# One long branch per chunk of rows, or short ones: layer one of a mixture-of-experts kernel in four parts

## The chip, the core and the metric

One Trainium2 chip, one of its NeuronCores. Five engines run their own instruction streams and meet at semaphores: PE multiplies matrices, ACT and DVE compute element by element, POOL issues the row gathers and scatters, SP issues the other transfers. The metric is device time of one execution in microseconds (us). [...]

## The reference, cut to what matters

Eight batches of linear attention (random features, 8 heads, 576 positions) give 4608 rows of 512 numbers. Each row then goes to one of 8 experts, the one with the largest gate logit:

```python
for e in range(E):                       # E = 8
    mask = expert_idx == e
    xe = x[mask]                         # rows of 512
    h = np.maximum(xe @ w1[e], 0.0)      # w1[e]: 512 x 1024
    ye = h @ w2[e]                       # w2[e]: 1024 x 512
    out[mask] = gate_w[mask, None] * ye
```

How many rows an expert gets is known only when the kernel runs.

## The kernel before, in words

The first 310 us hold the attention, the routing, 256 rows of one expert and the first chunk. After that the experts' rows are taken in chunks of up to 384 (`T3`), t = 0, 1, 2, ...; a chunk belongs to one expert, and its last chunk holds what is left. The number of rows of chunk t lies in the flags as `r` (row 4), written by the routing; each engine loads it into a register (`reg`, L909) and branches on it.

A step (`step`, L1109) does chunk t. **Layer one** makes the 1024 hidden values in eight groups f of 128: 12 matmuls each for wide chunks (`l1`, L967: high and low parts of weights and rows), then ACT takes the relu and DVE the rest of it (`hid`, L992, L993). Chunks of at most 192 rows use `l1_both` (L974, L976: 8 matmuls per group, high and low rows side by side) and `hid_both`: ACT copies, DVE adds, ACT and DVE split (L1001, L1002, L992, L993). Four banks of PSUM (`p_1`) are used in turn, so a fifth group waits for the first one's `hid`. **Layer two** (`l2`) makes the output in blocks of 128 rows, 24 matmuls each (L886), or 16 where a block has at most 64 rows (L1029). Since each hidden group is one step of its sums, a block's last matmuls wait for the last group's `hid`. ACT scales the output (`out2`, L1080), POOL scatters it (L1061).

Beside it, the rows of chunk t+1 are brought into place: gathered by POOL (L923), reshaped through memory by SP (`move`, L942, L944), transposed by DVE and split by ACT and DVE (`xtrans`, L951, L57, L51), in three thirds. A wide chunk does a third after groups 1, 3 and 5; a slim chunk does all three ahead of its own layer one. Where the expert changes, ACT and DVE split the next weights (`change`: w1 when layer one has read the old ones, w2 at the start of the next step).

The size is chosen once per chunk (`cases`, L1034 to L1048): a tree of branches ends in one of six bodies, for 384, 320, 256, 192, 128 and 64 rows, each with all of layer one and all of layer two. The bodies stand one behind the other in every engine's stream, in that order. On PE a matmul stands as one row in the program and is two records in the trace, a weight load (PEld) and the matmul (PE). In such records with their closing branches the six bodies have 337, 322, 290, 210, 178 and 162, about 1,510 per chunk. The order of instructions on each engine is the order in which the code is written.

Of the kernel before, what the change touches and what calls it, by code (L numbers as in the profile page):

```python
# [18 lines left out]
P = 128  # L19
# [14 lines left out]
T2 = 2 * P  # L34
A3 = 3
T3 = A3 * P
HT = P // 2
# [7 lines left out]
ET = mybir.EngineType  # L45
# [371 lines left out]
class Routing:  # L417
# [99 lines left out]
    def step(self, name, product, f):  # L517

        v = {}
        def made(bank):  # L520
            v["o"] = product(bank)
        def step():
            if "o" not in v:
                made(self.bank(name))
            f(v["o"])
        step.product = made
        return step
# [263 lines left out]
class Experts:  # L791
# [2 lines left out]

    NC, NF, T2 = DM // P, F // P, T2
    WE = (ET.DVE, ET.Activation, ET.SP)

    def __init__(self, tc, ctx, rt, xs, w1, w2, out, ident, ps):
        self.tc, self.nc, self.ctx, self.rt, self.ps, self.ident = tc, tc.nc, ctx, rt, ps, ident
# [203 lines left out]
        for h, l, k in self.homes2(slice(f, f + w), n):  # L1003
            self.high_low(h, l, y[:, :, k])

    def wide(self, t, n):
        for f in range(self.NF):
            if t == 0:
                self.split(2, (f,))
            self.l1(t, f, n)  # L1010
            self.hid(f, n)
            if t > 0 and f in (1, 3, 5):
                self.xtrans(t + 1, f // 2)

    def slim(self, t, n):
        for a in range(A3):
            self.xtrans(t + 1, a)
        w = 2 if n <= P else 1
        for i in range(self.NF // w):
            for b in range(w):  # L1020
                self.l1_both(t, w * i + b, self.p_1[i % 4][:, b * 2 * n:(b + 1) * 2 * n], n)
            self.hid_both(i, w * i, w, n)

    def l2(self, a, half=False):
        s, p = slice(a * P, (a + 1) * P), self.p_2[a]
# [5 lines left out]
            else:  # L1031
                self.triple(p, self.hb[:, 0, c, s], self.hb[:, 1, c, s], c)

    def cases(self, r, first):  # L1034


        def body(n):
            first(n)
            a = (n - 1) // P
            self.l2(a, n % P > 0)  # L1040
            for b in range(a - 1, -1, -1):
                self.l2(b)

        self.either(r > T2, lambda: self.either(r > T3 - HT, lambda: body(T3), lambda: body(T3 - HT)),
                    lambda: self.either(r > T2 - HT, lambda: body(T2),
                                        lambda: self.either(r > P, lambda: body(T2 - HT),
                                                            lambda: self.either(r > HT, lambda: body(P),
                                                                                lambda: body(HT)))))  # L1048

    def either(self, cond, one, other):  # L1050
        with self.tc.If(cond) as c:
# [17 lines left out]
    def out2(self, t, a, r):  # L1069
        nc, p, g, i = self.nc, self.p_2[a], self.gate(t, a), A3 * t + a  # L1070

        def half(y):
            nc.scalar.copy(self.yt[:HT], p[HT:])
            nc.vector.tensor_tensor(out=self.yt[:HT], in0=p[:HT], in1=self.yt[:HT], op=ALU.add)
            nc.vector.tensor_scalar(out=y[:HT], in0=self.yt[:HT], scalar1=g[:HT], scalar2=None, op0=ALU.mult)

        def both():
            y = self.y()
            v = self.reg(4, t, T3, (ET.Activation, ET.DVE))
            self.either(v > a * P + HT, lambda: nc.scalar.activation(y, p, AF.Copy, scale=g), lambda: half(y))  # L1080
            self.scatter(y, self.idx[:, i:i + 1])

        if a:
            with self.tc.If(r > a * P):
                both()
        else:
            both()
# [5 lines left out]
    def change(self, t, n):  # L1093
        def f():
            self.split(n)
            self.next(t, n)
        self.when(self.reg(0, t, 1, self.WE), f)

# [8 lines left out]
        self.change(t, 1)  # L1107

    def step(self, t, following):  # L1109
        self.t = t  # L1110
        if 0 < t < NCH - 2:
            self.gather(t + 2)
        if t == 0:
            self.wide(t, T3)
            self.l21()
            for a in range(A3):
                self.xtrans(1, a)
            self.cases(self.reg(4, t, T3, (ET.PE,)), lambda n: None)
            self.gather(2)
            self.next(0, 2)  # L1120
        else:
            self.cases(self.reg(4, t, T3, (ET.PE, ET.Activation, ET.DVE)),
                       lambda n: self.wide(t, n) if n > T2 - HT else self.slim(t, n))
        if t + 1 < NCH:
            self.weigh(t + 1)
        self.nc.gpsimd.drain()
        following()
        r = self.reg(4, t, T3, (ET.Activation, ET.DVE, ET.Pool))
        for a in range(A3 - 1, -1, -1):
            self.out2(t, a, r)  # L1130
# [111 lines left out]
```

## Time and profile before

| | us |
|---|---|
| time, median of 3 runs | 724.16 (720.52 to 725.4) |
| profiled execution: its own time | 723.94 |
| its span, first to last instruction | 722.2 |
| PE busy | 671.8 (93%) |
| ACT / DVE / POOL busy | 363.9 / 380.8 / 267.2 |

The execution has 13 chunks. Their layer one starts on PE at 264 (t = 0), 311, 345, 381, 412, 447, 482, 516, 559, 579, 613, 647 and 695 us. By the shapes of the matmuls t = 3 takes the 320 body, t = 8 the 192 body, t = 12, the last, the 64 body, the ten others the 384 body.

How to read the rows: a line of the timeline has the start in us from the span's start, the length, engine, source line, operation, result and operands, how many were merged (x), and in brackets how long the engine was idle just before and what ended that. "issue" is idle time in which it waited for nothing that the profile shows. The DMA queue q8 of kind "instruction" carries PE's program.

### The profile page before, as it was taken

The page shows a single profiled execution, that of the slowest core. Times are in us where ns is not written, and L with a number is a line of the kernel's source. Part 1 is how long each engine was busy: PE and PEld are TensorE (multiplying, and loading weights), DVE is VectorE, ACT ScalarE, POOL GpSimd, SP SyncE. Part 2 cuts the span into 40 slices and gives each one's busy share as a digit, 9 for nine tenths or more (in the row PEclk, how much of TensorE's full clock was granted, in tenths as well). Part 3 has the DMA queues.
Part 4 walks back from the last instruction along what each step waited for, and adds up shares of the span by engine and source line. Part 5 has one row for each costly group of instructions (what it writes and reads, how often), then busy time and mean ns, then how long its engine had stood idle before and what let it go on. Part 6 is the DMA issues. An engine that isn't in the chain of part 4 may idle for free. (4 is left out here: it accounts for less than half of the span.)

```text
span 722.2 us, 18842 instructions
## 1 busy us (share of the span) xinstructions
PE 671.8 (93%) x7011; PEld 607.5 (84%) x7011; DVE 380.8 (53%) x789; ACT 363.9 (50%) x1142; POOL 267.2 (37%) x489
## 2 busy tenths in 40 slices
PE   8999999999999999999999998999994999999645
PEld 5999999999889879888979796989893997979545
DVE  4788888888878787331404560505542570505111
ACT  4999999999989564221312531213521551312110
POOL 5554557877777761331212032030033031221300
PEclk9999999999999999999999999999998999999956
DMA  7673653844852328643333465413366374313100
GB/s 211 205 224 93 214 178 101 256 131 142 272 210 71 96 63 248 228 130 105 108 74 104 132 210 163 122 63 95 135 202 168 91 277 142 97 54 90 49 4 8
DMA packets 92869, 100.54 MB, mean 139 GB/s; under 512 B 28702, under 2 KB 73246, under 8 KB 92064
## 3 DMA queue, kind: packets, MB, share of 16 engines
q1 hardware_dynamic: 85216, 79.27, 36.7%
q0 software_dynamic: 6800, 19.03, 8.2%
q8 instruction: 89, 1.46, 0.9%
q14 instruction: 76, 0.62, 0.3%
q10 hardware_dynamic: 688, 0.16, 0.1%
HBM read 72.12 MB, written 29.77 MB: 141 GB/s over the span
## 5 line engine op out<-in xcount | busy, mean ns | idle before, releaser
L967 PE MATMUL p<-xb,w1p 128*128 128x384 f32 (+1 forms) x1056 | 185.5, 335 | 9.3 <-issue 4.8
L967 PEld LDWEIGHTS p<-xb,w1p 128*128 128x128 f32 x1056 | 181.8, 189 | 13.9 <-issue 7.0
L1061 POOL DMA_INDIRECT out_dram<-ys,idx x38 | 38.2, 1004 | 349.6 <-ACT ys L1080 141.5
L993 DVE SCALAR_TENSOR_TENSOR hb<-p,hb 128x384 fp32r<-128x384 f32 (+1 forms) x88 | 46.9, 541 | 159.8 <-ACT hb L992 159.5
L886 PE MATMUL p<-w2p,hb 128*128 128x512 f32 x552 | 127.1, 389 | 0.0
L886 PEld LDWEIGHTS p<-w2p,hb 128*128 128x128 f32 x552 | 103.6, 188 | 21.5
L191 DVE TENSOR_REDUCE mx<-pp 128x8 f32<-128x1024 f32 x64 | 78.0, 1218 | 10.9 <-PE pp L185 10.2
L199 ACT ACTIVATE qp<-pp,mx 128x128 f32<-128x128 f32 x256 | 76.9, 432 | 0.0
L199 ACT ACTIVATE kp<-pp,mx 128x128 f32<-128x128 f32 x256 | 73.8, 382 | 5.7 <-DVE de L283 1.8
L185 PE MATMUL pp<-omt,th 64*128 64x128 f32 x1024 | 72.1, 281 | 0.2 <-ACT qp_-1_320 L199 0.2
L992 ACT ACTIVATE hb<-p 128x384 fp32r<-128x384 f32 (+1 forms) x88 | 41.3, 478 | 59.6 <-PE p L967 59.6
L185 PEld LDWEIGHTS pp<-omt,th 64*128 64x128 f32 x1024 | 63.4, 191 | 0.3 <-ACT qp_-1_320 L199 0.3
L1080 ACT ACTIVATE ys<-p,gt 128x512 f32<-128x512 f32 x23 | 15.8, 688 | 85.0 <-PE p L886 84.5
L886 PE MATMUL p_1tr<-w2p,hb 128*128 128x512 f32 x240 | 56.4, 390 | 0.0
L211 POOL TENSOR_TENSOR k<-kp 128x256 f32<-128x256 f32 x64 | 46.5, 727 | 25.8 <-ACT kp L199 20.8
L886 PEld LDWEIGHTS p_1tr<-w2p,hb 128*128 128x128 f32 x240 | 44.9, 188 | 9.0
L274 PE MATMUL nu<-kva,qt 128*64 128x73 f32 x1008 | 46.3, 233 | 0.7 <-issue 0.7
L176 DVE COPY th<-tr 128x512 f32<-128x512 f32 x63 | 43.3, 688 | 5.3 <-PE tr L168 3.2
L974 PE MATMUL p<-xb,w1p 128*128 128x384 f32 (+1 forms) x64 | 23.0, 424 | 24.8 <-issue 24.8
L243 ACT COPY qt<-t 128x512 f32<-128x512 f32 x64 | 41.9, 654 | 2.3 <-PE t L168 1.8
L274 PEld LDWEIGHTS nu<-kva,qt 128*64 128x64 f32 x1008 | 36.8, 136 | 5.1 <-issue 0.9
L225 PE MATMUL kf<-kp,v 128*64 128x128 f32 x512 | 39.7, 275 | 0.1
(386 smaller groups left out, 1087.4 us busy)
## 6 DMA issues: line engine op xcount, KB each, us to landing
w1s<-in_moe_w_dram SPq DMA_DIRECT2D x5, 2048.0 KB, 9.2
w2s<-in_moe_w_dram SPq DMA_DIRECT2D x5, 2048.0 KB, 10.5
xq<-chunk_rows SPq DMA_DIRECT2D x52, 192.0 KB, 4.2
v<-in_v_dram SPq DMA_DIRECT2D x32, 256.0 KB, 5.8
token_rows<-x SPq DMA_DIRECT2D x8, 1024.0 KB, 8.6
k<-in_k_dram SPq DMA_DIRECT2D x31, 256.0 KB, 5.3
q<-in_q_dram SPq DMA_DIRECT2D x31, 256.0 KB, 5.6
chunk_rows<-xgm SPq DMA_DIRECT2D x7, 768.0 KB, 3.6
```

What stands on the lines that cost most here:

```text
L176: self.nc.vector.tensor_copy(t.rearrange("p n (a t) -> p a n t", a=2), s[("tr", h)])
L185: nc.tensor.matmul(o[:, a, n, :], t[r, n, :], self.om[r], start=True, stop=True)
L191: self.nc.vector.tensor_reduce(out=mx, in_=s[("pp", h)], axis=AX.X, op=ALU.max, negate=True)
L199: self.nc.scalar.activation(o[:, j, :], p[:, a, 2 * n + i, :], AF.Exp, bias=mx[:, a, 2 * n + i:2 * n + i + 1])
L211: nc.gpsimd.tensor_tensor(out=k2, in0=kp[:, :2, :], in1=kp[:, 2:, :], op=ALU.add)
L225: nc.tensor.matmul(pkv[c * D:(c + 1) * D, :M], vv, kk, start=n < 2, stop=n > 2)
L243: self.nc.scalar.copy(qt.rearrange("p n (a t) -> p a n t", a=2), s[("t2", h)])
L274: nc.tensor.matmul(o[r, j, :], qt[:, j, r], kva[:, h if h >= 0 else 2 * j + a, :], start=True, stop=True)
L886: self.nc.tensor.matmul(p, x, w[:, c, :], start=c == 0 and x is h and w is self.w2h, stop=c == self.NF - 1 and x is l)
L967: self.nc.tensor.matmul(o, w[:, c, k], x[:, c, :], start=i == 0, stop=i == len(ops) - 1)
L992: self.nc.scalar.activation(h, p, AF.Relu)
L993: self.nc.vector.scalar_tensor_tensor(out=l, in0=p, scalar=0.0, in1=h.bitcast(F32), op0=ALU.max, op1=ALU.subtract)
```

## The change

The choice of a size is taken four times in layer one, once for two groups each (`layer1`, `choose`), and then again for each block of layer two (`layer2`). The body of a part is two groups at one of the six widths: 49 records (48 and a branch) at 384, 320 and 256 rows, 33 or 34 at 192, 128 and 64. A part is 246 records with its branches, layer two about 250, a chunk some 1,240. The thirds of `xtrans` follow parts 0, 1 and 3 at every width. Chunk 0 keeps its straight layer one (`first`) and loses two branches in `out2`.

```diff
-    def wide(self, t, n):
+    def first(self, n):
         for f in range(self.NF):
-            if t == 0:
-                self.split(2, (f,))
+            self.split(2, (f,))
+            self.l1(0, f, n)
+            self.hid(f, n)
+
+    def wide(self, t, g, n):
+        for f in (2 * g, 2 * g + 1):
             self.l1(t, f, n)
             self.hid(f, n)
-            if t > 0 and f in (1, 3, 5):
-                self.xtrans(t + 1, f // 2)
-
-    def slim(self, t, n):
-        for a in range(A3):
-            self.xtrans(t + 1, a)
+
+    def slim(self, t, g, n):
         w = 2 if n <= P else 1
-        for i in range(self.NF // w):
+        for f in range(2 * g, 2 * g + 2, w):
+            i = f + g // 2 if w == 2 else f
             for b in range(w):
-                self.l1_both(t, w * i + b, self.p_1[i % 4][:, b * 2 * n:(b + 1) * 2 * n], n)
-            self.hid_both(i, w * i, w, n)
+                self.l1_both(t, f + b, self.p_1[i % 4][:, b * 2 * n:(b + 1) * 2 * n], n)
+            self.hid_both(i, f, w, n)
...
-    def cases(self, r, first):
...
+    def layer1(self, t):
+        r = self.reg(4, t, T3, self.CE)
+        for g in range(self.NF // 2):
+            body = lambda n: self.wide(t, g, n) if n > T2 - HT else self.slim(t, g, n)
+            self.choose(r, [T3 - i * HT for i in range(T3 // HT)], body)
+            if g != 2:
+                self.xtrans(t + 1, (0, 1, None, 2)[g])
+
+    def choose(self, r, ns, body):
+        if len(ns) == 1:
+            return body(ns[0])
+        self.either(r > ns[1], lambda: body(ns[0]), lambda: self.choose(r, ns[1:], body))
+
+    def layer2(self, t):
+        r = self.reg(4, t, T3, (ET.PE,))
+        one = lambda a: self.l2(a) if t == 0 else \
+            self.either(r > a * P + HT, lambda: self.l2(a), lambda: self.l2(a, True))
+        for a in range(A3 - 1, 0, -1):
+            with self.tc.If(r > a * P):
+                one(a)
+        one(0)
...
@@ def step(self, t, following):
         if t == 0:
-            self.wide(t, T3)
+            self.first(T3)
             self.l21()
             for a in range(A3):
                 self.xtrans(1, a)
-            self.cases(self.reg(4, t, T3, (ET.PE,)), lambda n: None)
             self.gather(2)
             self.next(0, 2)
         else:
-            self.cases(self.reg(4, t, T3, (ET.PE, ET.Activation, ET.DVE)),
-                       lambda n: self.wide(t, n) if n > T2 - HT else self.slim(t, n))
+            self.layer1(t)
+        self.layer2(t)
```

**PE, before**: the end of the 192 body and the start of the next. Between the two stands the choice that a chunk of 128 or 64 rows reaches only by jumping over all that is above (`p` an output bank, `w2p` and `w1p` weights, `hb` hidden values, `xb` rows).

```order
L886 MATMUL p_6258<-w2p_6263,hb 128x512
L886 MATMUL p_6258<-w2p_6262,hb 128x512
L1051 UNCONDITIONAL_BRANCH
L1051 COMPARE_AND_BRANCH
L974 MATMUL p_6484<-xb_6271,w1p_6260 128x256
L976 MATMUL p_6484<-xb_6271,w1p_6261 128x128
```

**PE, with the change**: the end of a part's 384 body and the start of its 320 body.

```order
L968 MATMUL p_6485<-xb_6271,w1p_6261 128x384
L968 MATMUL p_6485<-xb_6271,w1p_6260 128x384 x4
L1059 UNCONDITIONAL_BRANCH
L1059 COMPARE_AND_BRANCH
L968 MATMUL p_6484<-xb_6271,w1p_6260 128x320
L968 MATMUL p_6484<-xb_6271,w1p_6261 128x320
```

A part ends at a branch after two groups, and the jump at its end passes 50 + 50 + 34 + 34 + 34 = some 200 records instead of the 1,160 that stood behind the whole 384 body; the last choice (64 rows) is reached past some 215 records, where it was past 1,340.

**PE, with the change, layer two**: the end of a block's half form, the way past that block, and the next block's choices (with the semaphores that are waited for).

```order
L1031 MATMUL p_1tr<-w2p_6262,hq 128x512
L1031 MATMUL p_1tr<-w2p_6263,hq 128x512
L1059 UNCONDITIONAL_BRANCH
L1054 UNCONDITIONAL_BRANCH [waits PE_49]
L1054 COMPARE_AND_BRANCH
L1059 COMPARE_AND_BRANCH
L887 MATMUL p_6259<-w2p_6262,hb 128x512
```

A chunk that skips a block goes by the row with the wait: PE waits there for its own earlier matmuls. No such wait stood between the layers before.

**DVE, before**: the start of the 64 body (`xq` the reshaped rows of the next chunk, `hs` and `hq` the hidden values on their way).

```order
L1051 UNCONDITIONAL_BRANCH
L951 STREAM_TRANSPOSE xg<-xq 128x512
L51 TENSOR_TENSOR xb_6270<-xg,xb_6270 128x4x128
L951 STREAM_TRANSPOSE xg<-xq 128x512
L51 TENSOR_TENSOR xb_6270<-xg,xb_6270 128x4x128
L951 STREAM_TRANSPOSE xg<-xq 128x512
L51 TENSOR_TENSOR xb_6270<-xg,xb_6270 128x4x128
L1002 TENSOR_TENSOR hs_6268<-p_6484,hs_6268 128x128
L993 SCALAR_TENSOR_TENSOR hq<-hs_6268,hq 128x2x64
```

**DVE, with the change**: the 64 body of part 0, what follows the part, and the start of part 1.

```order
L1059 UNCONDITIONAL_BRANCH
L1003 TENSOR_TENSOR hs_6268<-p_6484,hs_6268 128x128
L994 SCALAR_TENSOR_TENSOR hq<-hs_6268,hq 128x2x64
L1059 UNCONDITIONAL_BRANCH
L952 STREAM_TRANSPOSE xg<-xq 128x512
L51 TENSOR_TENSOR xb_6270<-xg,xb_6270 128x4x128
L1059 COMPARE_AND_BRANCH
L994 SCALAR_TENSOR_TENSOR hb<-p_6486,hb 128x384
```

The next chunk's transposes have moved from ahead of the slim chunk's hidden values to between them.

## Rows read from the trace of the kernel before

**Rows 1.** The page, part 1: busy time, share of the span, instructions of PE.

```profile
PE 671.8 (93%) x7011; PEld 607.5 (84%) x7011; DVE 380.8 (53%) x789; ACT 363.9 (50%) x1142; POOL 267.2 (37%) x489
```

**Rows 2.** PE's groups by shape, 310.3 to 722.2 us: busy, mean ns, idle before.

```profile
L967 PE MATMUL p<-xb,w1p 128*128 128x384 f32 x864 | 152.5, 335 | 6.8 <-ACTq L1090 3.8 <-issue 2.2 <-ACT ys L1080 0.7
...
L967 PE MATMUL p<-xb,w1p 128*128 128x320 f32 x96 | 15.8, 331 | 2.5 <-issue 2.5
L974 PE MATMUL p<-xb,w1p 128*128 128x128 f32 x32 | 12.4, 445 | 14.6 <-issue 14.6
L974 PE MATMUL p<-xb,w1p 128*128 128x384 f32 x32 | 10.6, 402 | 10.2 <-issue 10.2
```

**Rows 3.** PE's timeline: starts of chunks, ends of layer two.

```profile
446.94 0.97 PE L967 MATMUL p<-xb,w1p 128*128 128x384 f32 x4 [1.73 <-ACTq L1090]
449.13 16.22 PE L967 MATMUL p<-xb,w1p 128*128 128x384 f32 x92 [1.22 <-issue]
...
481.89 16.93 PE L967 MATMUL p<-xb,w1p 128*128 128x384 f32 x96 [0.17 <-issue]
...
538.13 11.04 PE L886 MATMUL p<-w2p,hb 128*128 128x512 f32 x48
...
579.37 16.83 PE L967 MATMUL p<-xb,w1p 128*128 128x384 f32 x96
...
669.62 11.04 PE L886 MATMUL p<-w2p,hb 128*128 128x512 f32 x48
...
708.93 5.85 PE L1029 MATMUL p<-w2p,hq 128*128 128x512 f32 x16
```

**Rows 4.** Stretches: busy by engine (instructions), granted clock, DMA share, GB/s.

```profile
17.50:260.60 243.10, 237.48 (x4810) 222.03 (x4807) 201.25 (x465) 221.12 (x842) 163.25 (x315) 1.00 0.53 163
...
549.20:559.40 10.20, 0.01 (x1) 0.04 (x1) 5.13 (x6) 2.54 (x4) 4.95 (x7) 0.67 0.42 126
559.40:570.30 10.90, 10.90 (x65) 10.90 (x66) 4.99 (x19) 4.86 (x20) 0.00 (x0) 0.84 0.20 74
570.30:579.40 9.10, 9.10 (x42) 7.53 (x42) 6.54 (x14) 5.88 (x14) 0.00 (x0) 1.00 0.54 117
...
695.20:708.90 13.70, 13.65 (x64) 13.68 (x65) 1.75 (x6) 1.72 (x6) 0.00 (x0) 0.50 0.01 2
```

**Rows 5.** PE's program queue, 17.5 to 260.6 us: packets, MB, share.

```profile
q8 instruction: 37, 0.61, 1.1%
```

**Rows 6.** The same queue, 478 to 480 us.

```profile
q8 instruction: 1, 0.02, 3.3%
```

**Rows 7.** The same queue, 549 to 559.4 us.

```profile
q8 instruction: 3, 0.05, 2.4%
```

**Rows 8.** The same queue, 677 to 695.3 us.

```profile
q8 instruction: 6, 0.10, 2.3%
```

**Rows 9.** ACT's timeline in chunks 8 and 12.

```profile
564.82 0.32 ACT L1001 COPY hs<-p 128x192 f32<-128x192 f32 x1
...
565.96 0.32 ACT L1001 COPY hs<-p 128x192 f32<-128x192 f32 x1
...
572.49 4.27 ACT L57 CAST w1p<-w1s 128x512 fp32r<-128x512 f32 x8 [0.74 <-PE p L1029]
...
680.82 0.69 ACT L1080 ACTIVATE ys<-p,gt 128x512 f32<-128x512 f32 x1 [4.75 <-PE p L886]
683.32 0.62 ACT L57 CAST xb<-xgm 128x512 fp32r<-128x512 f32 x1 [1.81 <-issue]
...
698.99 0.27 ACT L1001 COPY hs<-p 128x128 f32<-128x128 f32 x1 [10.32 <-PE p L974]
```

**Rows 10.** DVE's timeline in chunk 12.

```profile
684.58 1.07 DVE L951 STREAM_TRANSPOSE xgm<-xq 128x512 f32<-128x512 f32 x1
...
686.95 1.07 DVE L951 STREAM_TRANSPOSE xgm<-xq 128x512 f32<-128x512 f32 x1
...
699.95 0.29 DVE L993 SCALAR_TENSOR_TENSOR hq<-hs,hq 128x128 fp32r<-128x128 f32 x1 [0.38 <-ACT hq L992]
```

More of the change, by code (lines that the diff above doesn't have):

```diff
@@ L796 @@
     WE = (ET.DVE, ET.Activation, ET.SP)
+    CE = (ET.PE, ET.Activation, ET.DVE)
     def __init__(self, tc, ctx, rt, xs, w1, w2, out, ident, ps):
@@ L1032, in l2 @@
                 self.triple(p, self.hb[:, 0, c, s], self.hb[:, 1, c, s], c)
-    def cases(self, r, first):
[L1037 to L1048, printed above, removed]
+    def layer1(self, t):
[17 more added lines that the diff above has]
+        one(0)
     def either(self, cond, one, other):
@@ L1077, in both @@
         def both():
+            if t == 0:
+                self.store(p, g, self.idx[:, i:i + 1])
+                return
             y = self.y()
@@ L1109, in step @@
     def step(self, t, following):
-        self.t = t
         if 0 < t < NCH - 2:
```

## The prediction, made blind

> **What bounds the kernel now.** The page's first part says PE: busy 93% of the span, the other engines about half [rows 1]. A share over stages tells little, so the second look is at PE's groups by shape from chunk 1 on, with the idle time before each. All idle time that counts there stands before layer one: 6.8 us before the 384 shapes, 2.5 before 320, 10.2 before the 192 body and 14.6 before the 64 body, 34.1 in all [rows 2]. Nearly all has the releaser "issue": no semaphore was late. The third view, PE's timeline, shows where: at the starts of chunks, and there unevenly. A wide chunk starts 0.17 us after the layer two before it, or 0.00, or 1.73 [rows 3]; chunk 8 starts 10.2 us after it, chunk 12 14.6.
>
> The fourth view explains it: PE's program queue. In the straight code from 17.5 to 260.6 us it moved 37 packets while PE ran 4810 + 4807 records [rows 4, 5], one packet per 260 records. In the pause before chunk 8 it moved 3 packets, around the pause before chunk 12 six [rows 7, 8]. 18.3 us / 6 is 3.05 us per packet when each is waited for. So the pauses are program fetch: to reach the 64 body PE jumps over 1,337 records, over five packets of code. The jump past the other bodies at the end of a 384 body (1,165 records, 4.5 packets) happens too, but there a packet moves between 478 and 480 [rows 6] while PE still works on matmuls already in its queue until 481.7, and only 0.17 us shows. The reader is to see that the same jump costs nothing behind a full queue and its whole length when jumps follow each other with no matmul between.
>
> The pauses also lower the clock: granted mean 0.67 in the pause and 0.84 over chunk 8's layer one, 0.50 over all of chunk 12's, 1.00 again in layer two of chunk 8 [rows 4].
>
> **The change part by part.** All times below count from the end of the previous layer two.
>
> *Chunk 12 (64 rows).* Today: from 669.62 + 11.04 = 680.66 to 708.93 + 5.85 = 714.78 [rows 3], 34.1 us. With the change two chains run side by side. On PE, layer one and two have some 1,240 records, 4.8 packets; the first is there already, since layer two of chunk 11 stands right before it, so 3.8 x 3.05 = 11.6 us, then layer two's 16 matmuls, 5.85 at the low clock: 17.4. The wait where blocks are skipped comes in here; no row shows it, its bounds are 0.17 and 1.73 (smallest that is not zero and largest start of a wide chunk [rows 3]), 0.5 is taken as nearest to the small one because layer one's short matmuls are long through when the code arrives: 17.9. On ACT and DVE: ACT's first own work came 683.32 - 680.66 = 2.7 us in [rows 9]; a part's hidden values take from ACT's copy at 698.99 to DVE's end at 700.24, 1.25 us [rows 9, 10]; a third of the transposes 686.95 - 684.58 = 2.4 [rows 10]. The last hidden values now stand behind two thirds: 2.7 + 4 x 1.25 + 2 x 2.4 = 12.5, plus the new branches of ACT and DVE (0 to 1.8 in all, the latter the issue gap [rows 9]; 1.0 taken, between them), and 4 matmuls of 0.37: 15.0. PE is later. But its queue lets it take the first packets ahead of time, so I take 16.5 between the two: **17.6 us saved**, bounds 11 (every packet waited for from the start, at the 10.2 / 3 = 3.4 us of chunk 8's pause [rows 2, 7]: 4.8 x 3.4 + 5.85 + 0.5 = 22.7) and 19.
>
> *Chunk 8 (192 rows).* Today 538.13 + 11.04 = 549.17 to 579.37, 30.2 us [rows 3]. On PE 11.6 + 40 matmuls x 0.23 (11.04 / 48) = 20.8. On ACT and DVE a group takes 565.96 - 564.82 = 1.14 [rows 9]: 2.7 + 8 x 1.14 + 2 x 2.4 + 1.0 = 17.6, then the 4 matmuls that need the last group and the full block's 24, 28 x 0.23 = 6.4: 24.0. Here ACT and DVE are late next, not the code: **6.2 saved**. Behind it ACT's split of the next w1 (4.27 us, started 572.49 [rows 9]) moves from 8 us before the end of layer two to about 4 before it, and the w2 split after it delays chunk 9's first hidden values: 1.0 lost, bounds 0 and 3. Net **5.2**, bounds 2 (PE half its time idle, so 24 matmuls at 0.37 instead of 0.23) and 9.4.
>
> *Starts of the ten wide chunks after chunk 0.* Layer two's end now stands some 50 records ahead of the next head, so no packet far away is fetched. 6.8 + 2.5 = 9.3 us are there [rows 2]; 0.2 each may stay (as at 481.89 [rows 3]), 2.0: **7.3 saved**, bounds 4 and 9.3.
>
> *New joins.* Each wide chunk gets three inside layer one, one between the layers and two inside layer two: 10 x 6, and 2 in chunk 0. Each adds two branches or so, and the jump of 200 records stays within the next packet. Its cover: a 384 part keeps PE busy 16.9 / 4 = 4.2 us (320: 4.0), while the next packet needs 3.05; in straight code packets come ahead of their use (PE busy 237.5 of 243.1 us over 37 of them [rows 4, 5]); and behind a full queue a whole fetch left 0.17. So 0, which is the value at 579.37; the upper bound is 0.17 each, 10.5. If the cover went (a packet slower than 4.2 us), each crossing would show.
>
> First the row: before chunk 6 the head (a register load and seven branches and compares) shows no more than 0.17 us, fetch included [rows 3]. [...]
>
> *Moved work.* The third third of the transposes in wide chunks goes from behind group 5 to behind group 7: 2.4 us of ACT and DVE, covered by layer two's 16.5 us; no gather, transfer or scatter moves on POOL's or SP's queue. Without that cover the next chunk would start up to 2.4 later.
>
> **Sum.** 17.6 + 5.2 + 7.3 - 0 = 30.1 against the profiled execution's own 723.94: 693.8. The median of the runs is 0.2 above it, so **694 us**. With all good bounds 686, with all bad ones 717.
>
> **Rivals.** (1) The joins leak: 62 x 0.17 = 10.5, giving 704. For it: chunk 5 stopped for 1.22 us inside layer one [rows 3]. Against: starts of 0.00 and 0.17 with more branches. 14%. [...] (2) Slower: packets do not come ahead. Chunk 5's 1.22 us is PE running to the end of a packet whose follower was asked for too late. If every crossing did that, 10 chunks x 4.8 crossings x 1.22 = 59 us, giving 753; from 0.63 us per crossing (30.1 / 48) the kernel is slower than now. Against: a 384 chunk crosses packets today too, and only that once it shows. 6%. (3) ACT and DVE pay at every part what ACT paid at 683.32, 1.81 us of issue: 4 parts in chunks 8 and 12, 14 us, giving 708. Against: their code for a part is far smaller than a packet. 7%. (4) The change does not remove the waits: they belong to something else, a register or a semaphore, and stay, with some of the starts kept: 718 to 724. Against: six packets in one pause. 5%.
>
> **How the numbers follow.** The forecast has 68%, and its own range is 686 to 702. The range takes in rivals 1 and 3 with 3 us above them, and at the lower end 2 us for the case that PE keeps its high clock in chunk 12 (16 matmuls at 0.23 instead of 0.37): 684 to 711. A difference below 1% (717 to 731) is about what a measurement of this kernel cannot tell from none. Faster by more: 68 + 14 + 6 = 88%; same: 6%, from rivals 3 and 4; slower: 6%, rival 2.
>
> **What would show it.** Right: before the new layer one (`l1_both`) the idle time falls from 10.2 and 14.6 to under 3 us each, the 34.1 to under 12 in all; between the end of chunk 11's layer two and the end of the last lie 15 to 19 us; in chunk 8 PE waits for DVE's `hb` or `hq` instead of "issue"; layer one of wide chunks stays at 16.9 us; clock 1.00 through chunk 8. Wrong: "issue" gaps of 0.5 us or more between the four parts of wide chunks (rival 2), or of about 0.2 at all of them (rival 1).

## The result, and the profile after

The changed kernel takes 689.48 us (median of 4 runs, 688.47 to 691.62), the kernel before 724.78 beside it: a ratio of 0.9525, 95% interval [0.9476, 0.9574]. Timed a second time it was 690.39 us, ratio 0.9563 [0.9539, 0.9586]. 694 us were forecast, with a range of 684 to 711. The profiled execution took 690.08 us, its span is 688.4.

The page's first part, and PE's groups by shape from 307.1 us on (columns as in [rows 1] and [rows 2]):

```profile
PE 663.7 (96%) x7011; PEld 601.6 (87%) x7011; DVE 381.6 (55%) x789; ACT 364.1 (53%) x1142; POOL 268.3 (39%) x489
```

```profile
L968 PE MATMUL p<-xb,w1p 128*128 128x384 f32 x864 | 152.1, 335 | 1.7 <-DVE hb L994 1.1 <-issue 0.6
...
L968 PE MATMUL p<-xb,w1p 128*128 128x320 f32 x96 | 14.2, 309 | 0.0
L975 PE MATMUL p<-xb,w1p 128*128 128x384 f32 x32 | 10.6, 393 | 2.3 <-DVE hq L994 1.9 <-issue 0.4
L975 PE MATMUL p<-xb,w1p 128*128 128x128 f32 x32 | 10.2, 377 | 2.3 <-ACT hs L1002 1.4 <-issue 1.0
L1031 PE MATMUL p<-w2p,hq 128*128 128x512 f32 x32 | 9.8, 462 | 1.9 <-PEq L1054 1.5 <-DVE hq L994 0.4
```

Against [rows 2]: the idle time in front of layer one falls from 6.8, 2.5, 10.2 and 14.6 to 1.7, 0.0, 2.3 and 2.3 us, and "issue" is no longer the main releaser. PE does the same 7011 matmuls. PE's timeline, which answers to [rows 3] and [rows 4] together with the windows of chunks 8 and 12 below it (start, length, engine, line; in brackets the idle time before; the windows have the busy time of PE, PEld, DVE, ACT, POOL, then PE's granted clock, 1.00 and 0.50 the highest and the lowest value that the windows of this case show):

```profile
468.57 16.83 PE L968 MATMUL p<-xb,w1p 128*128 128x384 f32 x96
...
523.85 11.04 PE L887 MATMUL p<-w2p,hb 128*128 128x512 f32 x48
...
544.28 0.41 PE L975 MATMUL p<-xb,w1p 128*128 128x384 f32 x1 [1.92 <-DVE hq L994]
...
553.28 5.62 PE L887 MATMUL p<-w2p,hb 128*128 128x512 f32 x24
...
568.31 7.69 PE L968 MATMUL p<-xb,w1p 128*128 128x384 f32 x43 [1.06 <-DVE hb L994]
...
649.25 11.04 PE L887 MATMUL p<-w2p,hb 128*128 128x512 f32 x48
...
662.99 0.33 PE L975 MATMUL p<-xb,w1p 128*128 128x128 f32 x1 [0.96 <-issue]
...
666.65 0.45 PE L975 MATMUL p<-xb,w1p 128*128 128x128 f32 x1 [1.36 <-ACT hs L1002]
...
674.58 5.60 PE L1031 MATMUL p<-w2p,hq 128*128 128x512 f32 x16 [0.87 <-PEq L1054]
```

```profile
534.90:548.80 13.90, 10.99 (x64) 10.12 (x63) 7.54 (x20) 6.07 (x21) 4.46 (x7) 0.88 0.43 139
...
660.30:664.50 4.20, 3.24 (x30) 3.10 (x29) 0.89 (x3) 1.26 (x3) 2.47 (x3) 1.00 0.19 65
664.50:673.70 9.20, 7.84 (x37) 7.50 (x36) 4.35 (x8) 2.38 (x6) 2.14 (x5) 0.50 0.04 7
673.70:680.20 6.50, 5.61 (x17) 4.14 (x16) 2.30 (x4) 1.19 (x3) 0.00 (x0) 0.66 0.03 6
```

The reader is to see three things. A wide chunk (468.57) starts with no gap. Chunk 8 now reaches from 523.85 + 11.04 = 534.89 to 553.28 + 5.62 = 558.90, 24.0 us, and its longest wait is for DVE. Chunk 12 reaches from 660.29 to 680.18, 19.9 us, of which 3.2 are idle; from 664.5 to 673.7 its clock is 0.50, and layer one is there a row of weight loads: 7.50 us for 36, 0.21 each.

PE's program queue over chunks 1 to 12, in the kernel before (310.3 to 714.8 us) and in the changed one (307.3 to 680.2 us):

```profile
q8 instruction: 47, 0.77, 0.8%
q8 instruction: 61, 1.00, 1.1%
```

So the changed kernel moves more code, 61 packets instead of 47. What it saves is the waiting, 6.3 us in front of layer one instead of 34.1: its code is passed in short steps, and by these waits most of it is there when PE comes to it.

| stretch | before | after | forecast | measured |
|---|---|---|---|---|
| idle in front of and in the ten wide chunks' layer one, without chunk 9 after | 9.3 | 0.3 | -7.3 | -9.0 |
| chunk 8 | 30.2 | 24.0 | -6.2 | -6.2 |
| chunk 9 | 33.0 | 35.3 | +1.0 | +2.3 |
| chunk 12 | 34.1 | 19.9 | -17.6 | -14.2 |
| chunk 3 from its first matmul | 31.2 | 28.8 | 0 | -2.4 |
| behind the last layer two | 7.4 | 8.2 | 0 | +0.8 |
| up to layer one of chunk 0 | 271.3 | 268.3 | 0 | -3.0 |

These are -31.7 of the -33.8 us between the two spans; the rest is spread over the rows of layer one (16.83 instead of 16.93 where a gap stood in front) and their overlaps. The 3.0 in front of chunk 0 is not the change's: in the profiles of all twelve runs below layer one of chunk 0 starts at 267.2 to 269.5, those built from the kernel before among them (267.87, 267.42).

### The profile page after: what moved, and what is told of

The parts are those of the page before. It is cut to its first block, busy times and chain, and to the rows that moved or that the text cites. A ratio compares the mean times of both kernels' runs of the same rounds, so it can differ in the third digit from the quotient of the medians.

```text
span 688.4 us, 19220 instructions
## 1 busy us (share of the span) xinstructions
PE 663.7 (96%) x7011; PEld 601.6 (87%) x7011; DVE 381.6 (55%) x789; ACT 364.1 (53%) x1142; POOL 268.3 (39%) x489
## 5 line engine op out<-in xcount | busy, mean ns | idle before, releaser
L968 PE MATMUL p<-xb,w1p 128*128 128x384 f32 (+1 forms) x1056 | 183.6, 333 | 1.7 <-DVE hb L994 1.1
L887 PEld LDWEIGHTS p<-w2p,hb 128*128 128x128 f32 x552 | 103.6, 188 | 21.6
L212 POOL TENSOR_TENSOR ks<-k 128x128 f32<-128x128 f32 x64 | 29.2, 457 | 5.0
```

What stands on the lines that cost most here:

```text
L887: self.nc.tensor.matmul(p, x, w[:, c, :], start=c == 0 and x is h and w is self.w2h, stop=c == self.NF - 1 and x is l)
L968: self.nc.tensor.matmul(o, w[:, c, k], x[:, c, :], start=i == 0, stop=i == len(ops) - 1)
```

## The experiments

The theory: a pause is program fetch. A jump that lands in a packet that is not there costs a fetch, and in a chain of jumps each such landing does; matmuls that are still queued hide a part of it. The rivals: the price goes by the records passed; each branch costs something; the waits belong to something else.

**Order of the bodies.** Kernel before, the narrow body first:

```
-        self.either(r > T2, lambda: self.either(r > T3 - HT, lambda: body(T3), lambda: body(T3 - HT)),
...
+        ns = [HT * (i + 1) for i in range(T3 // HT)]
+        tree = lambda ns: body(ns[0]) if len(ns) == 1 else \
+            self.either(r < ns[0] + 1, lambda: body(ns[0]), lambda: tree(ns[1:]))
+        tree(ns)
```

> The kernel before, with the six whole bodies in the opposite order (64 rows first, 384 last). Each chunk still passes the same amount of foreign code, only on the other side of its own body. Theory (a jump is cheap when it is the last one behind full matmuls, and each landing of a chain of jumps has to be fetched): a wide chunk now passes five bodies, 1162 records, before its first matmul; at the 14.6 us / 1337 records of chunk 12 that is 12.7 us less some 2.5 us of queued matmuls, about 10 us for each of ten wide chunks: +95. Chunk 12 starts within 3 us (-12), chunk 8 passes 340 records instead of 949 (-6). About 800 us. Rival (what counts is the amount of code passed per chunk, wherever it lies): wide starts stay at 0 to 2 us, 705 to 725 us. In both, chunk 12's layer one stays at 13 to 14 us if half clock sets it, and falls under 8 us if code was what it waited for.

825.32 us, ratio 1.1407 [1.1385, 1.143]: 102 us slower, where some 77 were expected. PE's groups, and the timeline at chunk 4:

```profile
L967 PE MATMUL p<-xb,w1p 128*128 128x384 f32 x864 | 173.1, 365 | 112.8 <-issue 112.8
```

```profile
452.70 18.66 PE L967 MATMUL p<-xb,w1p 128*128 128x384 f32 x96 [19.26 <-issue]
```

The nine 384 chunks wait 112.8 us, 12.5 each, and run the first matmuls after it at a low clock (mean 0.74 from 452.7 to 460.0 us; 173.1 us busy instead of 152.5). No arithmetic changed, and a chunk passes as much foreign code as ever; it only has to pass it in a chain of jumps ahead of its body instead of in one jump behind it. The rival that goes by the amount of code per chunk falls, and so does the one that the waits are something else. That 12.5 is nearly the whole 12.7 expected without cover is chance, for the nine pauses run from 7.4 to 21.5 us though all pass the same 1162 records. Two of them, chunk 4's and chunk 11's (in the last two columns the share and the GB/s of the DMA engines):

```profile
433.40:452.70 19.30, 0.04 (x2) 0.01 (x1) 4.91 (x8) 4.94 (x9) 3.80 (x4) 0.57 0.67 241
758.10:765.40 7.30, 0.00 (x0) 0.00 (x0) 0.00 (x0) 0.69 (x1) 4.46 (x7) 0.65 0.14 43
```

Four packets of PE's program moved in the first and two in the second; over all ten wide chunks it is 3.7 to 5.0 us for each packet moved in a pause. The three longest pauses (15.1, 19.3 and 21.5 us) are those in which the DMA engines also moved new weights, at 241 to 279 GB/s. That this traffic makes a fetch slower is what the rows suggest; no run tests it. Chunk 12, whose code now follows layer two directly, took 15.7 us without any idle time:

```profile
801.10:805.00 3.90, 3.90 (x37) 3.90 (x35) 1.43 (x2) 1.30 (x2) 2.19 (x3) 0.96 0.18 67
805.00:811.00 6.00, 6.00 (x31) 6.00 (x30) 3.84 (x9) 2.33 (x8) 2.63 (x5) 0.50 0.02 0
```

Here 35 weight loads take 3.90 us at clock 0.96 (0.11 each) and 30 take 6.00 at 0.50 (0.20): PE is full, so 9.9 us is what its layer one takes where no code is waited for. Of the two figures expected (13 to 14, or under 8) neither came; the change's 13.4 (660.3 to 673.7) has both in it, 2.3 us of waits (0.96 and 1.36) and more of its loads at the half clock, 36 instead of 30.

**One half of the change.** Kernel before, with only layer two taken out of the bodies:

```
 def body(n):
     first(n)
-    a = (n - 1) // P
-    self.l2(a, n % P > 0)
-    for b in range(a - 1, -1, -1):
-        self.l2(b)
...
+        self.layer2(t)
```

> The kernel before with one half of the change: layer two leaves the bodies and branches by itself; layer one stays in six whole bodies, transposes stay where they were. Theory by distance (10.9 ns per record jumped in a chain): chunk 8 passes 580 records instead of 949, pause 6.3 instead of 10.2; chunk 12 passes 840 instead of 1337, 9.1 instead of 14.6; wide starts fall to 0 because layer two now stands right in front of the next head (-9.3); the jump of up to 770 records from layer one to layer two costs 0 to 0.2 in wide chunks and up to 3 in chunk 8: 706 to 710 us. Rival by number of jumps (two to reach the 192 body, four to reach the 64 body, as before): narrow pauses stay, 714 us. Rival (something else than code): 720 to 724 us.

737.97 us, ratio 1.0218 [1.0187, 1.0249]: slower than before by about 2%, which no theory expected. A wide chunk:

```profile
341.09 16.83 PE L967 MATMUL p<-xb,w1p 128*128 128x384 f32 x96
362.90 8.29 PE L886 MATMUL p_1tr<-w2p,hb 128*128 128x512 f32 x24 [4.98 <-issue]
```

The starts are at 0.0 as expected, but the pause has moved to between the layers, 1.55 to 4.98 us in each of the ten wide chunks, 28.5 us in all (with 1.16 shortly behind it in chunk 10). After the pauses of 2.68 us and more layer two starts at a low clock (here 8.29 us instead of 5.64, with a mean of 0.50 from 362.9 to 367.0 us). I had put the jump of up to 770 records there at 0 to 0.2. Chunk 8 took 25.0 us, 5.2 less than before, with the transposes where they had been: its gain does not come from their new place. Chunk 12 took 29.1 with a pause of 8.46 (9.1 expected by distance). So layer two apart brings nothing by itself; the short parts of layer one are what makes it pay.

**Dead code.** Changed kernel, with one body that is never taken ahead of the third part, then (second run) ahead of the first:

```
+        r = self.reg(4, t, T3 + HT, self.CE)
+        def never():
+            for k in range(32):
+                self.l1(t, 4, T3)
+            self.wide(t, 2, T3)
...
+            self.either(r > T3, never, rest) if g == 2 else rest()
```

> The changed kernel with one more body, never taken, in front of the third part of layer one of every chunk after chunk 0: 816 PE records that have to be jumped over (the register's comparison is with 384, which no chunk exceeds). Theory by distance: narrow chunks pay 8.9 us each, wide chunks 8.9 less the 4 us or so of queued matmuls: +5 each, some 755 us. Theory by landings (one far jump is one fetch, however far): narrow chunks +3 each, wide chunks 0 to 0.2 each: 695 to 699 us. Rival (code costs nothing, the gain came from the order of transposes and waits): 689 to 691 us.

735.29 us, ratio 1.0152 [1.013, 1.0173], some 45 us more than without it (689.48 and 690.39). Chunk 2, with the jump ahead of its second row:

```profile
343.15 8.51 PE L968 MATMUL p<-xb,w1p 128*128 128x384 f32 x48
354.34 8.56 PE L968 MATMUL p<-xb,w1p 128*128 128x384 f32 x48 [2.67 <-DVE xgm L952]
```

The program queue (packets, MB, share), from 343.2 to 354.4 us in chunk 2, in the same stretch of the changed kernel (340.2 to 351.4), and over chunks 1 to 12 (308.5 to 726.1, to set beside the changed kernel's 61):

```profile
q8 instruction: 3, 0.05, 2.6%
q8 instruction: 2, 0.03, 1.1%
q8 instruction: 84, 1.38, 1.6%
```

The pauses at this jump are 0.74 to 4.25 us, 24.1 in ten wide chunks, and what follows at a lower clock comes on top (after the pause of 4.25 us a mean of 0.50 for 4.6 us: 11.20 us for 48 matmuls instead of 8.56); chunk 8 took 28.8 us and chunk 12 25.6, 4.8 and 5.7 more. A jump over 3.1 packets moves one packet more in chunk 2, and about two more per chunk on average (84 instead of 61 in twelve chunks). So some of the passed code is not fetched, and neither the distance (755 us) nor the landing alone (695 to 699) gives the time. Nor do the queued matmuls hide the jump, as I had said they would; 2.4 us are left on average. The releaser named (DVE, ACT) is the last semaphore that came: the work of ACT and DVE for these chunks is that of the changed kernel, where PE does not wait for it.

> The changed kernel with the same dead body as in the earlier run (816 PE records never taken), but in front of the first part of layer one, behind layer two, instead of in front of the third part, behind layer one. Theory (what covers a jump is the time that the queued matmuls take, and behind layer two they last about as long as a fetch: before the change the jump past 1165 records cost 0 to 1.7 us there): wide chunks 0 to 1 us each, narrow ones 3 to 5 each, 698 to 708 us. Rival (the price goes by the records jumped over, wherever it is): 735 us as in the earlier run.

728.56 us, 1.0077 [1.005, 1.0104], 38 us more than the changed kernel timed beside it (690.39). The 384 shapes, and the program queue over chunks 1 to 12 (307.2 to 721.2 us):

```profile
L968 PE MATMUL p<-xb,w1p 128*128 128x384 f32 x864 | 159.8, 346 | 18.6 <-ACT w2p L57 6.8 <-issue 5.1 <-DVE hb L994 2.1
```

```profile
q8 instruction: 85, 1.39, 1.5%
```

The pauses at the ten wide starts are 0.81 to 3.75 us, 16.4 in all, 1.6 on average; chunk 8 took 29.8, chunk 12 26.6. Behind layer two the jump costs less than behind layer one, but far more than the 0 to 1 expected. The same number of packets moves in either place. My explanation by cover carries only a third of the price. In the kernel before, a jump past 1165 records in the same place left 0.93 on average [rows 2], and up to 2.53 (chunk 3), more than the 1.7 that I gave; what makes the difference (there the jump came first, here a register load stands ahead of it) was not tried.

**Two parts instead of four.**

```
-        for g in range(self.NF // 2):
+        for g in range(self.NF // 4):
...
-        for f in (2 * g, 2 * g + 1):
+        for f in range(4 * g, 4 * g + 4):
```

> The changed kernel with layer one in two parts of four groups instead of four of two: half as many joins, each part twice as long; a 384 chunk jumps some 390 records at each join instead of 197; the thirds of the transposes keep their places. Theory (one packet of some 260 records is read ahead, so a jump of 197 always lands in code that is there or on its way, a jump of 390 lands beyond it about every second time, and then costs the 2.6 us that the single jump over dead code cost behind layer one): 20 joins x 0.5 x 2.6 = 26 us more in wide chunks, 716 us. Rival (fewer joins are better, queued matmuls cover the jump): 687 to 691 us.

717.91 us, 0.9943 [0.9918, 0.9968]: of the gain almost nothing is left. The 384 shapes of layer one, which have the join in the middle, and the first block of layer two, which has the join behind layer one:

```profile
L968 PE MATMUL p<-xb,w1p 128*128 128x384 f32 x864 | 153.0, 335 | 5.6 <-DVE xg L952 1.7 <-DVE hb L994 1.4 <-ACT xb L57 1.1
...
L887 PE MATMUL p_1tr<-w2p,hb 128*128 128x512 f32 x216 | 55.8, 418 | 14.1 <-issue 14.0
```

In wide chunks PE waits 20.6 us at the joins (13 of 20 show a pause, 0.35 to 3.85 us; chunks 1 and 2 have none), and chunk 12 takes 22.6. The theory, that one packet is read ahead and a jump of 197 records stays in it while one of 390 often leaves it, gave 716. That the number came out is in part luck: 10 pauses of 2.6 us were expected, 13 of 1.6 came, and the rest lies in chunk 12 (2.7 us) and in a lower clock behind the pauses (55.8 us busy instead of 51.0). That the limit is one packet, and not another length between 197 and 390 records, the runs do not show.

**More branches.** Changed kernel, four conditions that always hold around each part:

```
-            self.choose(r, [T3 - i * HT for i in range(T3 // HT)], body)
+            self.deep(4, r, lambda: self.choose(r, [T3 - i * HT for i in range(T3 // HT)], body))
+    def deep(self, k, r, f):
+        if k == 0:
+            return f()
+        with self.tc.If(r > 0):
+            self.deep(k - 1, r, f)
```

> The changed kernel with four more nested conditions (always true) around each part of layer one, on PE, ACT and DVE: 16 compare-and-branch instructions more per chunk and engine, no jump, 16 records. Theory (branches are free behind queued matmuls): wide chunks unchanged, narrow ones up to 1 us each, 689 to 692 us. [...]

695.18 us, 0.9605 [0.9589, 0.9621], about 5 us more than the change. Chunk 2:

```profile
340.60 16.83 PE L968 MATMUL p<-xb,w1p 128*128 128x384 f32 x96
357.27 5.64 PE L887 MATMUL p_1tr<-w2p,hb 128*128 128x512 f32 x24
362.75 11.04 PE L887 MATMUL p<-w2p,hb 128*128 128x512 f32 x48
373.63 14.24 PE L968 MATMUL p<-xb,w1p 128*128 128x320 f32 x96
```

From 340.60 to 373.63 are 33.03 us, as in the changed kernel (340.17 to 373.19, 33.02), with 16 more compare-and-branch instructions in it: on PE they showed no time. Six of ten wide chunks are unchanged to 0.02 us. The loss is in chunk 8 (26.9 instead of 24.0), chunk 12 (21.6 instead of 19.9), and in four wide chunks that wait 0.5 to 2.4 us, three of them first for hidden values of ACT or DVE, which run the same branches. At the 0.17 us that rival 1 gives to a join, the 160 in ten wide chunks would have made 27 us.

**Four widths.** Changed kernel, a third less code in each part:

```
-            self.choose(r, [T3 - i * HT for i in range(T3 // HT)], body)
+            self.choose(r, [T3, T3 - HT, T2 - HT, HT], body)
```

> The changed kernel with four widths to choose from (384, 320, 192, 64; the next larger one is taken) instead of six. In these 13 chunks the same bodies run as before, but a part of layer one has some 163 records instead of 246. Theory A (chunk 12 waits for code: 3.2 us for each packet of 260 records): its layer one has two thirds of the code, 13.4 falls to about 9.5 us, and it saves 3 to 4 us; total 685 to 687. Theory B (chunk 12's layer one is set by 64 weight loads at half clock, 0.21 us each, 13.4 us): it stays within 1 us, total 688 to 691.

685.27 us, 0.9482 [0.9449, 0.9515]: faster than the change. Chunk 12 took 18.3 us, 1.6 less, its layer one 11.1 instead of 13.4; its middle:

```profile
661.00:667.70 6.70, 6.64 (x32) 6.45 (x31) 4.05 (x8) 2.29 (x6) 1.91 (x5) 0.50 0.02 4
```

PE is full there, 6.45 us for 31 loads at half clock. So theory A and theory B each have a part: PE's waits in layer one fall from 2.3 us to 0.5, and the half clock remains. ACT and DVE also pass fewer branches here, so how much of the gain is PE's code alone the run does not separate. The small "issue" gaps that the change left in chunks 4 and 9 (0.30, 0.32, 0.30) are gone as well; chunk 8 took 23.2, chunk 9 34.3.

**Clock in chunk 12.** Changed kernel, the 64 body (and the 128 body) multiplies 192 columns (m is 192):

```
-                self.l1_both(t, f + b, self.p_1[i % 4][:, b * 2 * n:(b + 1) * 2 * n], n)
+            self.l1_both(t, f, self.p_1[f % 4][:, :2 * m], m)
```

> The changed kernel with the 64 and 128 bodies multiplying 192 columns like the 192 body (the columns beyond the chunk's rows are left unread), one group at a time. It keeps PE longer at work in chunk 12. Theory B of the run with four widths (half clock and weight loads set chunk 12's layer one): with more columns the clock falls later or not at all; layer one takes 64 loads, or 64 matmuls of 0.1 to 0.17 us at full clock, 6.4 to 11 us and its waits, 1 to 3 us less than 13.4; 686 to 689 us. Theory A (code): 13 us still. In either case ACT and DVE have eight groups instead of four, 8 x 1.14 + 2 x 2.4 + 2.7 = 16.6 us to the last hidden values, which may give back all of it: 692 us at most.

692.85 us, 0.9588 [0.9555, 0.9622], not faster as a whole, but chunk 12 took 17.1 us instead of 19.9, with more arithmetic in it:

```profile
667.00:675.00 8.00, 6.11 (x40) 5.40 (x38) 4.66 (x10) 2.49 (x9) 2.54 (x5) 1.00 0.04 8
675.00:680.00 5.00, 3.90 (x16) 2.93 (x16) 2.45 (x9) 1.84 (x8) 0.00 (x0) 1.00 0.01 3
```

The clock stays at 1.00, a weight load takes 0.14 instead of 0.21, and layer two 3.90 us instead of 5.60. It is given back by the stretch behind the last layer two (10.0 us instead of 8.2: ACT and DVE end later) and by gaps of 0.8 to 1.4 us in chunks 4, 7 and 9.

**Place of the transposes.** Changed kernel, all three thirds behind the fourth part:

```
-            if g != 2:
-                self.xtrans(t + 1, (0, 1, None, 2)[g])
+        for a in range(A3):
+            self.xtrans(t + 1, a)
```

> The changed kernel with all three thirds of the next rows' transposes behind the fourth part, none between the parts. Theory (two thirds, 2 x 2.4 us, lie in ACT's and DVE's chain ahead of the last hidden values and make chunk 8 late; in wide chunks they are covered on either side): PE's waits for hq in chunk 8 (1.92 + 0.39) go, 2 to 3 us less, chunk 12 up to 1 us less (its 1.36 us wait for ACT); the wide chunks after the next one start with no wait since three thirds, 7.2 us, fit beside 16.5 us of layer two: 685 to 688 us. Rival (the transposes are needed in time: ACT's stores and the weights' splits stand in the same 16.5 us): wide chunks start up to 2 us late each, 692 to 710 us.

696.40 us, 0.9638 [0.961, 0.9665], slower than the change. Chunk 8 took 22.5 us, 1.5 less (2 to 3 expected), so two thirds in ACT's and DVE's chain did hold it up; chunk 12 took 19.0, 0.9 less. But chunk 9 took 39.8 (4.5 more), and 11.7 us stand behind the last layer two (3.5 more). DVE's timeline behind chunk 8:

```profile
554.03 1.08 DVE L952 STREAM_TRANSPOSE xgm<-xq 128x512 f32<-128x512 f32 x1
555.80 0.69 DVE L51 TENSOR_TENSOR xb<-xgm,xb 128x512 fp32r<-128x512 f32 x1 [0.69 <-ACT xb L57]
556.56 4.91 DVE L51 TENSOR_TENSOR w1p<-w1s,w1p 128x512 fp32r<-128x512 f32 x8
...
564.76 4.90 DVE L51 TENSOR_TENSOR w2p<-w2s,w2p 128x512 fp32r<-128x512 f32 x8 [1.12 <-ACT w2p L57]
569.58 1.94 DVE L994 SCALAR_TENSOR_TENSOR hb<-p,hb 128x384 fp32r<-128x384 f32 x4
```

The transposes push the two weight splits back, and chunk 9's first hidden values stand behind these: PE waits 3.77 us for `hb` at 570.27. The wide chunks elsewhere start without a gap, so there the place of the thirds is free.

**Versions that the runs point to.** Four widths, and the transposes only where a next chunk follows (`v`: there is one); then also the 192 columns of above:

```
-                self.xtrans(t + 1, (0, 1, None, 2)[g])
+                self.when(v, lambda: self.xtrans(t + 1, (0, 1, None, 2)[g]))
```

> The kernel with four widths, with the transposes skipped where no next chunk follows, and the 64 body as in the changed kernel. Chunk 12 has two thirds (2 x 2.4 us) less on ACT and DVE ahead of its last hidden values, but PE at half clock is later there: 0 to 0.5 us; the tail loses a third, 0.5 to 1 us; 0 to 2 us given back by branches on ACT and DVE: 684 to 687 us.

689.98 us, 0.9555 [0.953, 0.9581]: nothing left of the four widths' gain. Chunk 12 took 17.3 us, 1.0 less than with four widths alone, but chunk 8 24.5 and chunk 9 37.1 (23.2 and 34.3 there). A condition around each third now stands in ACT's and DVE's chain there; that it is the cause is likely, not shown. The tail behind the last layer two is 8.1 us, not shorter than the change's 8.2.

> The kernel with four widths, with two more edits that the runs point to: the 64 body multiplies 192 columns (which kept the clock at 1.00 through chunk 12, 17.1 us instead of 19.9), and the transposes are skipped where no next chunk follows (in the last chunk they stand ahead of the last hidden values and of the last stores; the tail behind the last layer two was 7.4 us before the change, 8.2 after, 10.0 with 192 columns, 11.7 with all transposes last). From 685.3: chunk 12 18.3 to about 16, tail to about 7.5, and 0 to 2 us lost to a branch more per third on ACT and DVE: 682 to 685 us. Rival (the extra branches make late hidden values in wide chunks, as four more per part did): 686 to 690.

684.88 us, 0.9479 [0.9456, 0.9502]. Chunk 12 took 14.3 us at clock 1.00, and 7.7 us stand behind it; chunks 8 and 9 lose as above (24.3 and 37.6). It is no faster than four widths alone, whose interval it shares; both are faster than the change (0.9563 beside it). Four widths with 192 columns and without the condition was not run.

> The changed kernel itself, timed beside the versions above: 689.5 us (0.9525 of the kernel before); its own profile again shows how far single waits differ between two executions: chunk 12 19.9 us, chunk 8 24.0 us, wide chunks 33.0 us, each within 1 us.

690.39 us, 0.9563 [0.9539, 0.9586]. Its profile has chunk 12 at 19.8, chunk 8 at 24.0, chunk 9 at 35.4 us, a wait of 0.58 us in chunk 4 at the same place as before (0.30 in the first) and no other in wide chunks but 9: in both executions the waits stand at the same places of the program.

## Why the prediction was right, point by point

- **What bounds it.** Right. Program fetch along jumps was the cause of the pauses: an opposite order of the same bodies cost 102 us, never-taken code 38 to 46. Too quick was "no semaphore was late": for 4.5 of the 9.3 us at the wide chunks [rows 2] names ACT as releaser. That those were fetch too the run with layer two apart shows: ACT's work is the same there, and every wide chunk starts without a gap.
- **Starts of wide chunks.** 7.3 forecast, 9.0 found; nothing of the 0.2 each stayed. The half with layer two apart shows the step by itself: all starts at 0.0. But what I had read into the 0.17 of chunk 6, that a far jump behind a full queue is all but free, is wrong as a rule: elsewhere it left 2.8 (layer two apart), 2.4 and 1.6 us (dead code). The change does not rest on that rule, since its jumps are short; had it not cut layer one, the sum would have failed by its sign. Nor was 1.73 the largest start: chunk 3's was 2.53 [rows 2].
- **Chunk 8.** 24.0 forecast and measured, and PE's longest wait is for DVE's `hq`, as said. That the figures agree to a tenth is in part luck: with two thirds, 4.8 us, out of ACT's and DVE's chain it took 22.5, only 1.5 less, and with a third less code 23.2, so ACT and DVE do not set it alone. The clock was not 1.00, as the sign of being right had it, but 0.88 over its layer one. Chunk 9 lost 2.3 instead of 1.0, within the bounds of 0 and 3, and by the mechanism named: its hidden values stand behind the w2 split (PE's 1.06 at 568.31), and 0.6 us of joins.
- **Chunk 12.** The term that failed: 16.5 forecast, 19.9 measured (15 to 19 was the sign of being right), 14.2 saved instead of 17.6. I let the fetch of 3.8 packets (11.6 us) stand for PE's side and called its matmuls "long through when the code arrives". At half clock they are not: a part's 16 loads at 0.21 take 3.3 us, more than the 3.05 of a packet, and with 2.3 us of waits layer one took 13.4 us instead of 11.6. The price was in the rows: 64 matmuls in 13.65 us at clock 0.50 [rows 4]. Of the 3.4 us missing, 1.8 are this, 1.4 the step from PE's 17.9 down to 16.5, for which no row spoke, and 0.4 the wait where blocks are skipped (0.5 taken, 0.87 measured); layer two gave 0.25 back. The order with the narrow body first shows layer one without code waits (9.9 us), the 192 columns show chunk 12 without the half clock (17.1), four widths and 192 columns without the transposes show it with little of either (14.3).
- **Joins.** 0 forecast; 0.9 us in three places, gone with four widths. Rival 1 (10.5) falls, and with 160 further branches in ten wide chunks PE's time did not move in six of them, and three of the other four wait first for ACT or DVE.
- **Moved third.** 0 in wide chunks, right. In the last chunk, where nothing follows, it does not hold up the last stores either: ACT's copy begins 0.04 us after layer two's end and POOL's scatter 2.7 us after it, before the change and after it. The 0.8 us behind the last layer two lie behind the scatter's start; their cause is open.
- **Not in the sum.** Chunk 3 gained 2.4: the pause of 2.53 in front of it had also cost clock in its layer one (a mean of 0.71 in its first 3.4 us; 15.85 us, now 14.24), and there was a wait for `hq`. A pause can cost more than its length.
- **The sum.** The spans differ by 33.8 us, and 30.1 were forecast. That they lie so close is in part luck: chunk 12, chunk 9 and the end took 5.5 us more than forecast; wide starts, chunk 3 and the rows behind gaps took 6.2 less, and 3.0 in front of chunk 0 are not the change's.
- **Rivals 2 to 4.** No "issue" gap of 0.5 us stands in wide chunks of the first profile, one of 0.58 in the second; ACT shows 1.6 us of issue once in chunk 8, not at every part; the waits did not stay. The chances of 6, 7 and 5% were not too small for this change, but rival 2's price is real two hundred records further: two parts lost 28 of 34 us.

## What to carry to other kernels

Where a program chooses among bodies at run time, count the records that each jump passes: behind queued matmuls, jumps of about 200 records on PE showed 0.9 us in all in ten wide chunks, and from 390 on a pause of 0.3 to 5 us stood at most of them; a chain of five jumps with no matmul between cost 7 to 21 us. Put what is common behind short choices instead of inside long bodies (689.48 us instead of 724.78 here), offer fewer variants if a slightly wider one serves (685.27 us with four widths), and put the order of the tree among the things to measure (825.32 us with the narrow body first). A narrow stage may be faster with more columns, where that keeps the clock up (the last chunk 17.1 us with 192 columns at clock 1.00, 19.9 with 64 at 0.50 in most of layer one); look at the granted clock in the window before costing its matmuls.

## What the runs showed of the hardware that was not expected

- Program code that is never executed made a kernel 38 to 46 us slower: 816 records per chunk, one jump over each block. About two packets more per chunk moved, of the 3.1 passed.
- The changed kernel moved more program code than the one before, 61 packets instead of 47 over chunks 1 to 12, and waited less for it: 6.3 us in front of layer one instead of 34.1.
- The same bodies in the opposite order: 723 to 825 us. One and the same chain of jumps took 7.4 to 21.5 us, longest (15.1 to 21.5) where the DMA engines also moved new weights, at 241 to 279 GB/s.
- 128 x 192 columns instead of 128 x 64 in the last chunk: 17.1 instead of 19.9 us, as the clock stayed at 1.00 instead of 0.50 and a weight load fell from 0.21 to 0.14 us.
- Compare-and-branch instructions on PE behind queued matmuls showed no time at all (16 in 33.03 us, against 33.02 without), while with the same 16 on ACT and DVE the narrow chunks took 1.7 and 2.9 us more.
